# RWKV-7 recurrence with a four-expert mixture: the second inverse product moved into the first one's stretch, and three orders restated

## The chip, the cores and the metric

The kernel runs on one core of a Trainium2 chip. The metric is the device time of one execution in microseconds (us), as the median of several runs.

## What is computed

Inputs are r, k, v, w, a, b of shape (4, 8, 768, 40), and for the mixture domain_probs (3072, 4), w1 (4, 320, 1024) and w2 (4, 1024, 320), all in float32. Cut to what matters, the reference is:

```python
for t in range(S):                       # state: (B, H, D, D), starts at 0
    y[:, :, t] = einsum('bhd,bhde->bhe', rt, state)
    Sa = einsum('bhde,bhe->bhd', state, at)
    state = state * wt[:, :, None, :] - einsum('bhd,bhe->bhde', Sa, bt) \
            + einsum('bhd,bhe->bhde', vt, kt)
x = y.transpose(0, 2, 1, 3).reshape(B * S, H * D)
p = domain_probs / (domain_probs.sum(-1, keepdims=True) + 1e-09)
for e in range(4):
    out += p[:, e:e + 1] * (maximum(x @ w1[e], 0) @ w2[e])
```

## The kernel before

**Chunks and units.** The recurrence over time is done in chunks of 64 steps, so that most of it becomes matrix products. A unit is one chunk of two of the four batches (all 8 heads): 12 chunks times 2 pairs are 24 units, numbered u. Inside a chunk the steps depend on each other through a triangular system per head. Its inverse is put together from 32-wide blocks: the diagonal blocks are solved step by step on GpSimd, and two products join them.

**The parts of a unit** are Python generators, each yield being a place where another part can be put in between:

- `within` (L402) is what needs no state. y1: the decays are turned (`turn_raw`, tile rawW) and multiplied up by a scan (tile G, L439). y2: pg (TensorE transposes), then gp and its reciprocal on VectorE. y3: n_tok, k_tok, AT, VT, RT, on VectorE. y4: transposes pNT and pKT, copied by ScalarE. y5: the scores pc, masked into VC by VectorE (`causal`, L400). y6: the matrix F from pfe. y7: pe, masked into ET. y8: pev, copied into EV.
- `substitute` (L542) solves the diagonal blocks of F: copies into blocks (two on VectorE, two on ScalarE, L547), a transpose and two operations on M (VectorE), then 48 small operations on GpSimd (tile Z, L580 and L593).
- `merge` (L599) joins the blocks. y1: Qc and QTc (VectorE transposes of Z), and four copies into QT (GpSimd). y2: the first product pY with four ScalarE copies into Yq. y3: the second product pQ with four ScalarE copies into QT. Both products go through `two_heads` (L616).
- `step` (L636) brings in the state. y1: prn, then RH (VectorE sums, L654) and SN (ScalarE copies, L659). y2: psat with the copies SaT and SX. y3: pxr with the mask into SX and the copies RS. y4: pdy, the output Y and the new state. y5: Y goes to xT, for most chunks by 12 DMAs on SP (L744).

**The mixture** of a finished chunk (256 tokens) is a list `todo` of pieces, for each expert: ups(e, 0), down_1 of the expert before, ups(e, 1), and down_2 of the expert before with add_h of this one. An ups is `up_last` (64x64 tiles, 16 records) and `up_main` (128x128, 16 records), then a Relu on ScalarE into hs. `lead()` (L981) issues the up_last of the next piece ahead of the rest. down_1 and down_2 are products over hs and its sums (tiles p, 24 and 32 records), added with the gate into osb on VectorE (L789, L791). The piece list lags, so an up never reads an xT that was just made.

**Buffers.** PSUM has five banks for the recurrence (tag big) and three for the mixture (tag mm): an up takes two of the three, down_1 one, down_2 two.

**Order.** The loop over u (L1100) calls the generators of units u, u+1 and u+2 in turn, with `gap(n)` in between, which runs pieces of the mixture: two per gap from u = 5 on. From there on an iteration traces, on TensorE: pe(u+1), pxr(u), gap 0, pg(u+2), pev(u+1), pdy(u), gap 1, pNT, pKT and pc of u+2, prn(u+1), pY(u+1), gap 2, pQ(u+1), pf(u+2), lead, psat(u+1), gap 3. The planner of the language orders each engine's instructions by priority, which is the place in the code, and by readiness as it reckons it. An instruction given to `keep_in_program_order` is pinned behind everything that was traced on its engine before it. Matmuls go through `stated` (L70), which pins them where `in_order[0]` is true: in the preparation and for u up to 5 (L1101). `within` has a local `pin` that pins for the first units only. DMAs of weights are pinned on SP; `later` holds the 16 moves of rawV and rawR, given out in small portions after pieces of the mixture (`begin_later`, L965). TensorE's records stand under the helper's lines L76 (matmul) and L79 (transpose), so one goes by the tile names.

Of the kernel before, what the change touches and what calls it, by code (L numbers as in the profile page):

```python
# [1 line left out]

# [13 lines left out]
def kernel(  # L16
# [38 lines left out]
    nc = tc.nc  # L55

    B, H, S, D = r.shape
    E, DM, F = moe_w1.shape
    P = 128
    L = 64  # L60
    Q = 32
    NC = S // L
    NJ = H // 2
    NF = F // P
    NU = NC * B // 2
    DT = DM - 2 * P

    in_order = [False]
# [16 lines left out]
    def big(name):  # L85
# [6 lines left out]
        out=ident[:], in_=ident[:], pattern=[[1, P]], compare_op=ALU.is_equal, fill=0.0,  # L92
# [5 lines left out]
    for t, n, op in ((upf, L, ALU.is_gt), (diagf, Q, ALU.is_equal)):  # L98
        nc.vector.memset(t[:], 1.0)
        for q in range(P // n):  # L100
            o = slice(q * n, (q + 1) * n)
            nc.gpsimd.affine_select(
                out=t[o], in_=t[o], pattern=[[1, n]], compare_op=op, fill=0.0, base=0, channel_multiplier=-1,
# [75 lines left out]


    EARLY = 5

    class Unit:
        pass

    units = []

    def begin(u):
# [3 lines left out]
        q.start, q.end = q.c == 0, q.c == NC - 1  # L192
        q.apart = u >= EARLY + 2
        q.n = {}
# [44 lines left out]
    def turn_raw(out, t):  # L239

        return nc.vector.transpose(
            out=out.rearrange("p n (x two) -> p n two x", two=2),
            in_=t.rearrange("p n (two e) -> p n two e", two=2)[:, :, :, 0:Q],
        )
# [92 lines left out]
    def quarter(q):  # L337
        return slice(Q * q, Q * q + Q)

    def of_slot(x, s):  # L340

        return x.rearrange("p (j s) e -> p j s e", s=2)[:, :, s, :]
# [30 lines left out]
    def of_d_half(x, r):  # L373

        return x.rearrange("p (jj four) e -> p jj four e", four=4)[:, :, slice(1, 3) if r else slice(0, 4, 3), :]
# [7 lines left out]
    def quadrants(p, lo, order, out_cols, *terms):  # L383


        for j, s, i in order:
            for n, term in enumerate(terms):
                row, col, at, lhsT, rhs = term(j, s, i)
                matmul(
                    out=p[row][half(col), lo + at * out_cols:lo + (at + 1) * out_cols], lhsT=lhsT, rhs=rhs,  # L390
                    start=(n == 0), stop=(n == len(terms) - 1),
                )
        return [by(x[:, lo:lo + NJ * out_cols], out_cols) for x in p]

    def causal(to, data):
        mask = mask_up[:, None, :].to_broadcast([P, data.shape[1], L])
        if len(to.shape) == 4:
            mask = mask_up[:, None, None, :].to_broadcast([P, 2, 2, L])
            data = data.rearrange("p (jj two) t -> p jj two t", two=2)
        return nc.vector.copy_predicated(out=to, mask=mask, data=data)  # L400

    def within(q):  # L402

        n = q.n

        def pin(ins, also=False):
            if q.u <= PADDED or also:
                tc.keep_in_program_order(ins)
# [3 lines left out]
        q.G = Gv = G[:, 0:2 * NJ * L].rearrange("p (c t) -> p c t", t=L)  # L412
        ahead = G[:, 1:2 * NJ * L + 1].rearrange("p (j i t) -> p i j t", i=2, t=L)
        for i in range(2):
            pin(turn_raw(ahead[:, i], n["rawW"][:, NJ * i:NJ * i + NJ, :]))
        q.gl = sb.tile([P, 2 * NJ, 1], FP32, name="gl", tag="gl", bufs=4)
        pin(nc.vector.tensor_tensor(out=q.gl[:], in0=G[:, L::L][:, :, None], in1=first[:, :, 0:1], op=ALU.mult))
        pin(nc.vector.memset(Gv[:, :, 0:1], 0.0))
# [16 lines left out]
        if q.u == 1:  # L435
# [4 lines left out]
            out=G[:, 0:2 * NJ * L], data0=G[:, 0:2 * NJ * L],  # L440
# [22 lines left out]
        def causal_scores(VT):  # L463
            pc = quadrants(banks("pc"), 0, BY_TOKENS, L, lambda j, s, i: (
                d_half(j, s), i, j, of_slots(VT, d_half(j, s), j, i, D), of_slots(q.RT, d_half(j, s), j, i, D),
            ))
            for r in range(2):
                pin(causal(of_d_half(q.VC[:, :, D:D + L], r), pc[r]), q.start)

        q.K, q.N = k_tok(), n_tok()  # L470
        ins = nc.vector.scalar_tensor_tensor(
            out=q.N[:, :, 0:D], in0=n["B"][:], scalar=-1.0, in1=gp[:], op0=ALU.mult, op1=ALU.mult,
# [126 lines left out]
    def merge(q):  # L599


        Qc = sb.tile([P, H, Q], FP32, name="Qc", tag="q", bufs=2)
        QTc = sb.tile([P, H, Q], FP32, name="QTc", tag="q", bufs=2)
        tc.keep_in_program_order(nc.vector.transpose(out=dealt(Qc[:]), in_=q.Z))  # L604
        tc.keep_in_program_order(
            nc.vector.transpose(  # L606
                out=QTc[:].rearrange("p h r -> p (h r)"), in_=Qc[:].rearrange("p h c -> p (h c)"),
            )
        )
        q.QT = QTs()  # L610
        for i in range(P // Q):
            ins = nc.gpsimd.tensor_copy(out=q.QT[quarter(i), :, quarter(i % 2)], in_=QTc[quarter(i)])  # L612
            tc.keep_in_program_order(ins)
        yield

        def two_heads(name, lhsT, rhs, to):  # L616
            p = big(name)
            for n in range(NJ):
                for r in range(2):
                    matmul(  # L620
                        out=p[half(r), n * 2 * Q:(n + 1) * 2 * Q], lhsT=lhsT[half(r), 2 * n:2 * n + 2, :],
                        rhs=rhs[half(r), 2 * n:2 * n + 2, :], start=True, stop=True,
                    )
            for r in range(2):
                for y in range(2):
                    src = p[quarter(2 * r + y), 0:H * Q].rearrange("p (n two t) -> p n two t", two=2, t=Q)[:, :, y, :]
                    nc.scalar.copy(out=of_slot(to[quarter(2 * r)], y), in_=src)  # L627

        Y = Ys()
        two_heads("pY", q.below, QTc, Y)  # L630
        yield

        two_heads("pQ", Qc, Y, q.QT[:, :, quarter(1)])
        yield

# [327 lines left out]
    todo, last, later, stores = [], [], [], []  # L963

    def begin_later(n):  # L965
        for move in later[:n]:
            tc.keep_in_program_order(move(nc.sync))
        del later[:n]
# [12 lines left out]
    def lead():  # L981
        if todo and hasattr(todo[0], "lead"):
            todo[0].lead()

    def run(gen, n=99):
        if gen is None:
            return
        for _ in range(n):
            if next(gen, gen) is gen:
                break  # L990
# [19 lines left out]
    ws = [within(units[u]) for u in range(3)]  # L1010
# [24 lines left out]
    m, s = merge(units[0]), begin_step(0)  # L1035
# [38 lines left out]
    m, s = merge(units[1]), begin_step(1)  # L1074
# [23 lines left out]
    sums_at.update({4 * 4 + 3: 2, 4 * 5 + 0: 3, 4 * 5 + 1: 2, 4 * 5 + 2: 3})  # L1098
    sum_ops = (None for e in range(E) for _ in add_weights(e))
    for u in range(1, NU):  # L1100
        in_order[0] = u <= EARLY  # L1101
        q = units[u]
        m = s_next = w = w_next = iter(())
        if u + 1 < NU:
            m, s_next = merge(units[u + 1]), begin_step(u + 1)
            w_next = ws[u + 1]
        if u + 2 < NU:
            w = ws[u + 2]

        def gap(n, pieces=None):  # L1110
            at = 4 * u + n
            run(sum_ops, sums_at.get(at, 0))
            mix((1 if at in sparse else 2) if pieces is None else pieces)

        early = u < EARLY
        if early:
            begin_later(len(later))
        ahead = u + 3 < NU and u in range(EARLY, EARLY + 3)
        if ahead:
            go(load_raw(begin(u + 3), "W"))  # L1120
        if early:
            lead()
        run(w_next, 99 if early else 1)
        run(s, 1)
        gap(0)


        if early:
            run(s, 1)
        run(w, 1)  # L1130
        if not early:
            run(w_next)
            run(s)

        if early:
            run(w, 1)
            gap(1, 2 if u + 1 == EARLY else None)
            run(s)
        if u == 1:
            mixture_of_unit(q)  # L1140
        elif q.bp:
            mixture_of_chunk(units[u - 1:u + 1], chunks_x[q.c])
        if not early:
            begin_later(len(later))
            run(w, 1)
            run(m, 1)
            gap(1)

        if u + 3 < NU:
            go(load_raw(units[u + 3] if ahead else begin(u + 3), "A" if ahead else "WA"))  # L1150
            load(units[u + 3], "WBKV")
            later.extend(load_raw(units[u + 3], "VR"))
        run(w, 2)

        soon = u in (2, 3, 4)
        if soon:
            run(w, 1)
        if early:
            run(m, 1)
        else:  # L1160
            run(s_next, 1)
            run(m, 1)
        if soon:
            substitute(units[u + 2], nc.gpsimd)
        gap(2)

        if not early:
            run(m, 1)
        if not soon:
            run(w, 1)  # L1170
        if not early:
            lead()
            run(s_next, 1)
        if not soon and u + 2 < NU:
            substitute(units[u + 2], nc.gpsimd)
        if early:
            run(w, 1)
        if u + 3 < NU:
            ws.append(within(units[u + 3]))
            run(ws[u + 3], 1)  # L1180
        if early:
            run(m, 1)
            run(s_next, 1)
            run(m)
            gap(3, 1)
            run(s_next, 1)
        else:
            gap(3)
        s = s_next
    mix(len(todo))  # L1190
# [30 lines left out]
```

## Time and profile before

| | |
|---|---|
| median of 3 runs | 1102.67 us (1099.94 to 1104.25) |
| profiled execution | 1102.3 us |
| its span, first to last instruction | 1100.6 us |
| mean granted TensorE clock | 0.991 |
| busy PE, DVE, ACT, POOL | 1070.0, 756.6, 353.0, 502.9 us |
| chain that ended last, PE's share | 81% |
| DMA, mean over the span | 111 GB/s |

PE is TensorE's matmuls and PEld its weight loads, DVE is VectorE, ACT ScalarE, POOL GpSimd, SP the queue that issues DMAs. A line of a timeline gives the start and the duration in us, engine, source line, operation, output tile and input tiles, shapes and count, and in brackets the idle time just before it with what ended it. A line of waits gives engine and tile, what was waited for, the sum in us, the number of waits and the longest.

### The profile page before, as it was taken

What the parts mean: (1) busy time and instruction counts of PE and PEld (TensorE: products, weight loads), DVE (VectorE), ACT (ScalarE), POOL (GpSimd) and SP (SyncE); (2) the same over time, 40 slices, a digit from 0 to 9 for tenths busy, and PEclk for the clock granted to TensorE, in tenths of its full rate; (3) what the DMA queues carried; (4) which work ended last, traced back from release to release, by engine and by line L of the source; (5) the groups of instructions that cost most, each with busy time, mean ns of one, the idle gap of its engine ahead of it and who ended that gap; (6) DMA issues with size and microseconds to landing.
All of it is one profiled execution on the core that took longest, in us unless ns stands there. A gap on an engine that the chain in (4) does not pass through costs nothing.

```text
span 1100.6 us, 38528 instructions
## 1 busy us (share of the span) xinstructions
PE 1070.0 (97%) x16102; PEld 955.8 (87%) x16102; DVE 756.6 (69%) x1551; ACT 353.0 (32%) x956; POOL 502.9 (46%) x1274
## 2 busy tenths in 40 slices
PE   6799899999999999999999999999999999999998
PEld 6677788789998999898999989989998989988887
DVE  7766668887777776767767768767767677543343
ACT  2432444223233233243233242332332432321110
POOL 5106677753463653743734635636537437430000
PEclk9799999999999999999999999999999999999999
DMA  7776545425345363354353444443552532222320
GB/s 117 226 247 138 136 103 117 119 55 136 98 111 127 98 140 97 94 146 103 93 144 94 102 121 104 116 120 84 127 123 65 147 85 67 98 69 82 104 76 13
DMA packets 268868, 122.18 MB, mean 111 GB/s; under 512 B 213736, under 2 KB 242072, under 8 KB 268696
## 3 DMA queue, kind: packets, MB, share of 16 engines
q1 hardware_dynamic: 265416, 119.12, 43.0%
q8 instruction: 127, 2.08, 0.8%
q10 hardware_dynamic: 3280, 0.61, 0.3%
q14 instruction: 45, 0.37, 0.1%
HBM read 111.79 MB, written 3.93 MB: 105 GB/s over the span
## 4 chain that ended last, share of the span: by engine, by line
PE 81%; DVE 7%; POOL 5%; ACT 3%; issue 2%; DMA 1%; SPq 0%; ACTq 0%; DVEq 0%; POOLq 0%
PE ph L76 35%; PE p L76 28%; POOL Z L593 3%; PE pdy L76 3%; PE psat L76 2%; PE pxr L76 2%; POOL Z L580 2%; PE prn L76 1%; PE pfe L76 1%; PE pQ L76 1%; PE po L76 1%; PE pc L76 1%; DVE Z L590 1%; PE pY L76 1%; DVE M L553 1%
## 5 line engine op out<-in xcount | busy, mean ns | idle before, releaser
L76 PE MATMUL ph<-xT,w1p 128*128 128x256 f32 (+3 forms) x3040 | 446.3, 377 | 4.0 <-issue 3.9
L76 PEld LDWEIGHTS ph<-xT,w1p 64*64 64x64 f32 (+1 forms) x3040 | 338.5, 162 | 72.7 <-issue 29.0
L593 POOL TENSOR_TENSOR Z<-Z 128x31 f32<-128x31 f32 (+7 forms) x704 | 260.0, 369 | 55.2
L897 DVE TENSOR_TENSOR a<-hs 128x512 f32<-128x512 f32 x220 | 151.8, 707 | 104.7 <-ACT hs L778 104.7
L580 POOL TENSOR_TENSOR Z<-M,Z 128x62 f32<-128x62 f32 (+7 forms) x352 | 144.1, 409 | 132.3 <-DVE M L569 106.4
L778 ACT ACTIVATE hs<-ph 128x512 f32<-128x512 f32 (+1 forms) x208 | 115.3, 564 | 226.5 <-PE ph L76 225.4
L76 PE MATMUL p<-sums,a 128*128 128x160 f32 x1056 | 164.9, 299 | 0.0
L76 PEld LDWEIGHTS p<-sums,a 128*128 128x128 f32 x1056 | 152.8, 190 | 2.2
L791 DVE SCALAR_TENSOR_TENSOR osb<-p,gate,osb 128x320 f32<-128x320 f32 (+1 forms) x243 | 108.1, 481 | 57.8 <-PE p L76 53.6
L550 POOL COPY below<-F 32x256 f32<-32x256 f32 x48 | 22.8, 475 | 198.7 <-ACT F L506 197.0
L76 PE MATMUL p<-w,a 128*128 128x160 f32 x704 | 105.9, 301 | 0.2 <-ACT hs L778 0.2
L76 PE MATMUL p<-w,hs 128*128 128x160 f32 x704 | 102.9, 299 | 0.0
L76 PEld LDWEIGHTS p<-w,hs 128*128 128x128 f32 x704 | 100.2, 190 | 2.2
L76 PEld LDWEIGHTS p<-w,a 128*128 128x128 f32 x704 | 98.3, 190 | 3.0 <-ACT hs L778 3.0
L612 POOL COPY QT<-QTc 32x256 f32<-32x256 f32 x96 | 51.7, 539 | 76.9 <-DVE QTc L606 67.7
L553 DVE STREAM_TRANSPOSE M<-blocks 128x1024 f32<-128x1024 f32 x24 | 47.4, 1977 | 38.1 <-ACT blocks L547 37.9
L700 ACT COPY RS<-pxr 64x256 f32<-64x256 f32 x88 | 32.2, 366 | 105.2 <-DVE SX L400 43.1
L451 DVE RECIPROCAL gp<-gp 128x320 f32<-128x320 f32 x24 | 51.6, 2151 | 0.7
L535 ACT COPY EV<-pev 64x160 f32<-64x160 f32 x96 | 23.1, 286 | 89.7 <-PE pev L76 89.3
L604 DVE STREAM_TRANSPOSE Qc<-Z 128x256 f32<-128x256 f32 x24 | 15.0, 627 | 46.2 <-POOL Z L593 46.1
L627 ACT COPY QT<-pQ 32x128 f32<-32x128 f32 x96 | 24.6, 256 | 59.9 <-PE pQ L76 58.2
L659 ACT COPY SN<-prn 128x256 f32<-128x256 f32 x44 | 14.9, 372 | 78.6 <-DVE RH L654 78.6
(149 smaller groups left out, 1357.5 us busy)
## 6 DMA issues: line engine op xcount, KB each, us to landing
w1p<-in_moe_w_dram SPq DMA_DIRECT2D x95, 512.0 KB
w1p<-in_moe_w_dram SPq DMA_DIRECT2D x190, 64.0 KB
w<-in_moe_w_dram SPq DMA_DIRECT2D x4, 1280.0 KB
sums<-in_moe_w_dram SPq DMA_DIRECT2D x9, 512.0 KB
natW<-in_w_dram SPq DMA_DIRECT2D x48, 80.0 KB
natB<-in_b_dram SPq DMA_DIRECT2D x48, 80.0 KB
natK<-in_k_dram SPq DMA_DIRECT2D x48, 80.0 KB
out_dram<-osb SPq DMA_DIRECT2D x46, 80.0 KB
```

The source lines that it names most:

```text
L76: return stated(nc.tensor.matmul(**k))
L451: pin(nc.vector.reciprocal(out=gp[:], in_=gp[:]))
L535: nc.scalar.copy(out=of_slot(q.EV[half(p)], i ^ p)[:, :, 0:D], in_=pev[i][half(p)])
L553: ins = nc.vector.transpose(out=M[:], in_=cols)
L580: ins = eng.tensor_tensor(out=Z[:, 1:3, 0:n, j + 1:Q], in0=M[:, j:j + 2, None, j + 1:Q].to_broadcast([P, 2, n, m]), in1=Z[:, here, 0:n, j: ...
L593: eng.tensor_tensor(out=z[:, 0], in0=z[:, 0], in1=z[:, x], op=ALU.add)
L612: ins = nc.gpsimd.tensor_copy(out=q.QT[quarter(i), :, quarter(i % 2)], in_=QTc[quarter(i)])
L627: nc.scalar.copy(out=of_slot(to[quarter(2 * r)], y), in_=src)
L700: nc.scalar.copy(out=RS[half(s), x ^ s::2], in_=prs[x][half(s)].rearrange("p (j i) t -> p j i t", i=2),)
L778: nc.scalar.activation(out=h[:, i * HF // 2:(i + 1) * HF // 2, 0:n], in_=ph[i][:], func=ACTF.Relu,)
L791: nc.vector.scalar_tensor_tensor(out=to, in0=p, scalar=sc, in1=to, op0=ALU.mult, op1=ALU.add)
L897: nc.vector.tensor_tensor(out=t[:], in0=x, in1=y, op=op)
```

## The change

Five things are done, nearly all for u from 5 on.

1. **TensorE as stated**: `in_order[0]` is true for all u.
2. **Gap 1**: `lead()` is called, the next two pieces change places (down_1 comes before the rest of the up), and `merge` y1 (Qc, QTc, QT) is traced after the gap.
3. **The stretch before gap 2** is now pNT, pKT, pc, pY, prn, lead, pQ: `merge` y3 has come ahead of gap 2. Behind it `within(u+3)` y1 (the decay turn and scan) is traced, which stood before gap 3; its two turns are pinned from unit 8 on, so behind RH. For u = 1, prn and pY move ahead of pf and pe.
4. **Priority**: `sooner` lifts, by 200 places, the masking into VC (units from 7 on), the Yq copies, and the whole of `substitute`, which is called ahead of psat.
5. **Raw loads**: all moves left in `later` are issued before gap 3.

```diff
+    SOONER = 200
+    def sooner(wanted):
+        return tc.high_priority(offset=SOONER) if wanted else nullcontext()
...
-            pin(turn_raw(ahead[:, i], n["rawW"][:, NJ * i:NJ * i + NJ, :]))
+            pin(turn_raw(ahead[:, i], n["rawW"][:, NJ * i:NJ * i + NJ, :]), q.u > EARLY + 2)
...
-            for r in range(2):
-                pin(causal(of_d_half(q.VC[:, :, D:D + L], r), pc[r]), q.start)
+            with sooner(q.apart):
+                for r in range(2):
+                    pin(causal(of_d_half(q.VC[:, :, D:D + L], r), pc[r]), q.start)
...
-                    nc.scalar.copy(out=of_slot(to[quarter(2 * r)], y), in_=src)
+                    with sooner(name == "pY"):
+                        nc.scalar.copy(out=of_slot(to[quarter(2 * r)], y), in_=src)
...
-        in_order[0] = u <= EARLY
+        in_order[0] = True
...
         if not early:
             begin_later(len(later))
             run(w, 1)
+            lead()
+            todo[:2] = todo[1::-1]
+            gap(1)
             run(m, 1)
-            gap(1)
...
         if early:
             run(m, 1)
         else:
+            run(m, 1)
             run(s_next, 1)
+            lead()
             run(m, 1)
+            if u + 3 < NU:
+                ws.append(within(units[u + 3]))
+                run(ws[u + 3], 1)
         if soon:
             substitute(units[u + 2], nc.gpsimd)
         gap(2)
 
-        if not early:
+        if u == 1:
+            run(s_next, 1)
             run(m, 1)
         if not soon:
             run(w, 1)
+        if not soon and u + 2 < NU:
+            with sooner(not early):
+                substitute(units[u + 2], nc.gpsimd)
         if not early:
             lead()
             run(s_next, 1)
-        if not soon and u + 2 < NU:
-            substitute(units[u + 2], nc.gpsimd)
         if early:
             run(w, 1)
-        if u + 3 < NU:
+        if early:
             ws.append(within(units[u + 3]))
             run(ws[u + 3], 1)
-        if early:
-            run(m, 1)
-            run(s_next, 1)
+            if u > 1:
+                run(m, 1)
+                run(s_next, 1)
             run(m)
             gap(3, 1)
             run(s_next, 1)
         else:
+            begin_later(len(later))
             gap(3)
```

More of the change, by code (lines that the diff above doesn't have):

```diff
@@ L1 @@
-from contextlib import ExitStack
+from contextlib import ExitStack, nullcontext
 import concourse.bass as bass
```

## The prediction

> **What bounds the kernel now.** I read the page first, then TensorE's own waits, then the timelines of iteration u = 13 (from pe at 567.8 us to the next pe at 610.7 us).
>
> ```profile
> PE 1070.0 (97%) x16102; PEld 955.8 (87%) x16102; DVE 756.6 (69%) x1551; ACT 353.0 (32%) x956; POOL 502.9 (46%) x1274
> PE   6799899999999999999999999999999999999998
> PEclk9799999999999999999999999999999999999999
> ```
> TensorE is busy in every slice from about 250 us to the end, at full granted clock. By windows, PE is busy 675.28 of the 676.00 us from 267 to 943. So most of the time is work that the change keeps. What can go are waits that hide inside busy PE, and a few open ones before 267 us. TensorE's waits from 267 to 943:
>
> ```profile
> PEld p L76 <- ACT hs L778: 3.0, 13, 0.4
> PEld ph L76 <- PE pfe L76: 1.1, 2, 0.9
> PE ph L76 <- issue: 0.5, 1, 0.5
> ```
> The first is the one that repeats: 13 of 17 iterations, 0.23 us each. Its cause is on ACT and DVE:
>
> ```profile
> 590.86 1.32 DVE L439 TENSOR_TENSOR_SCAN G<-G,first 128x512 f32<-128x512 f32 x1
> 592.32 1.58 DVE L791 SCALAR_TENSOR_TENSOR osb<-p,gate,osb 128x320 f32<-128x320 f32 x4
> 593.82 0.76 DVE L400 COPY_PREDICATED VC<-mask_up,pc 128x256 f32<-128x256 int32 x2
> 595.82 0.55 DVE L654 TENSOR_TENSOR RH<-prn,EV 128x160 f32<-128x160 f32 x2
> ```
> ```profile
> 596.17 0.65 ACT L659 COPY SN<-prn 128x256 f32<-128x256 f32 x2 [4.20 <-DVE RH L654]
> 596.83 0.79 ACT L627 COPY Yq<-pY 32x128 f32<-32x128 f32 x3
> 597.65 1.09 ACT L778 ACTIVATE hs<-ph 128x512 f32<-128x512 f32 x2
> 605.59 0.81 ACT L547 COPY blocks<-F 32x256 f32<-32x256 f32 x2
> ```
> RH (the sum on prn) stands behind the next unit's decay scan and down_1's adds; ACT stands 4.20 us in front of SN; the three late Yq copies and then the Relu of the gap's hidden layer queue behind; the second accumulator of down_2 waits for a PSUM buffer that this Relu frees:
>
> ```profile
> 597.12 2.53 PE L76 MATMUL p<-w,a 128*128 128x160 f32 x16
> 600.67 0.62 PE L76 MATMUL pQ<-Yq,Qc 64*64 64x64 f32 x13
> ```
> The same 16 records take 2.34 us elsewhere, so about 0.2 us is stall. The last line above it (605.59) shows blocks after SaT and SX copies: the solve on POOL starts late and ends just in time, since DVE's Qc waits for it (next line) and pY follows 2.1 us after Qc starts.
>
> ```profile
> 588.92 0.63 DVE L604 STREAM_TRANSPOSE Qc<-Z 128x256 f32<-128x256 f32 x1 [2.38 <-POOL Z L593]
> ```
>
> [...]PEld is at 87%, PE at 97%, and the 3.0 us above stands under PEld while PE shows no idle.[...]
>
> **The change, part by part**, in us from pNT's start (588.63) unless said otherwise.
>
> *Order of TensorE.* In the trace the late PE order is already that of the code (pe pxr, gap 0, pg pev pdy, gap 1, pNT pKT pc prn pY, gap 2, pQ pf lead psat, gap 3), so pinning it costs nothing by itself. Its price is that no other piece fills in when an operand is late. The number of 128-to-64 switches stays four per iteration: 0.
>
> *Swap in gap 1.* After pdy come lead (0.95), down_1 (3.26), then the main part of up (3.65). down_1 needs a PSUM buffer beside lead's two: the last add of gap 0 ends at -8.85 (gp starts right after it), the buffer is needed about -7.0: 1.9 us to spare. a1 has been ready since gap 0. Its four adds on DVE (1.6 us) run 3.65 us earlier, out of RH's way. up's weights load goes 3.26 us later on SP; behind it are natB, natK and raw loads that now start at +6 or later anyway: 0.
>
> *pQ into the stretch.* Qc and QTc are pinned behind down_1's adds. Unit data of DVE (k_tok) end at -2.06 or -2.82, by turns; adds 1.6, Qc and QTc 1.05: QTc at +0.6 or -0.2. pY wants it at 0.44 + 0.53 + 0.51 = 1.48: 0.9 to spare. Z must then be done by about -0.5 (next part). Yq: pY ends 1.84, first copy about 2.05, four of 0.26 to 3.1. pQ comes after prn (0.93) and lead (0.87), at 3.64: 0.5 to spare; so ACT's work is hidden by these two, and without them it would cost 1.3 us as in iteration 1. One new wait: five PSUM buffers serve pNT, pKT, two pc, pY; prn's second bank must take pKT's, which ACT frees at 0.74 + 0.48 + 0.59 = 1.81, where prn wants it at 1.84. Bounds 0 and 0.1 us each; I take 0.06, 17 times: +1.0. pQ itself needs pc's buffer, and the copies into VC (0.76) now have priority: done by 2.4.
>
> *Scan behind RH.* Two turns of 0.41, gl 0.19, memset 0.07, scan 1.32, gl 0.18: 2.6 us of DVE leave RH's front; they issue no DMA, and rawW landed long before. RH follows prn at 2.9, SN at 3.6, the Relus come when gap 2's matmuls end. pg of that unit is 30 us later. The 0.23 us stalls go: **-3.0**. With QT copied by 5.3, psat (13.4) no longer comes 0.1 us behind it; psat to ph varies from 1.08 to 1.43, over its low end summed 1.4: **-1.4**. pf likewise, 0.53 to 0.62, summed: **-0.6**. Lead behind pf, the second line of waits: **-1.0** (its larger case, 0.9, in iteration 7).
>
> *Blocks with priority.* ACT's two copies (0.81) go ahead of SaT and SX, right after F: F ends about 13.9 (pQ's 0.4 is gone before it), M starts about 14.9 instead of 17.8. POOL's chain ends near -2.6 instead of +0.3. SaT and SX come 0.8 us later, hidden by gap 3 (6.9 us) before pxr.
>
> *Raw loads (SP).* The ten moves left are flushed before gap 3, 10 x 0.44 = 4.4 us of SP, ahead of its w1p load, which waits for gap 3's up anyway. DVE's waits for rawV (2 us) shrink; off the path: 0.
>
> *Iteration 1.* prn and pY go ahead of pf and pe, which then cover Yq: pQ's open wait of 1.33 goes but for some 0.4 (Yq's four copies against 1.0 us of pf, pe): **-0.9**. The wait for RT of unit 7 (0.94 at 246) stays.
>
> Sum: -3.0 - 1.4 - 0.6 - 1.0 - 0.9 + 1.0 = -5.9 us. Against the profiled execution (1102.3 us, span 1100.6) that is 1096.4; its median of runs is 1102.67, so 1096.8 there.
>
> **Rivals.**
> *A, the gain is eaten (1101).* For: pKT's buffer has no slack at all, and pQ's margin is 0.5 us, in an order that can no longer bend. If ACT holds NT back by 0.25 us more behind up's last Relu, prn waits 0.3 per iteration: -5.9 + 17 x 0.25 = -1.7. Against: ACT is busy 32%.
> *B, slower (1115).* QTc comes late. It decides from 1.4 us after pNT: pinned behind the adds, it also waits for whatever the planner puts before them on DVE. The AT turn and product (1.38 us, today behind VC) would bring QTc to 1.2 and 2.0; with 0.7 us of a DMA wait (today DVE waits 1.4 to 2.4 us for rawV) to 1.9 and 2.7, so pY stalls 0.5 and 1.3, on average 0.9, and the shortened slack on DVE adds pev's and psat's operands for perhaps 0.2 more: 17 x 1.1 = 18.7 on 1096.8. Against: DVE stood idle 1.4 to 2.4 us before Qc, and all of it must be used up first.
> *C, nothing moves (1102).* Steady PE order is the code's already; if the 0.23 us only moves to another buffer, the time stays with iteration 1's 0.9.
>
> **How the numbers follow.** A measurement of this kernel tells about 0.5% (5.5 us) from no change. Forecast case (1094 to 1099): 0.62, of which about 0.42 lies under 1097.2. A and C: 0.20. B: 0.18. So faster 0.42, same 0.40, slower 0.18. Low end: all waits gone, no new one, 1095.8, less the 2 us by which runs differ, 1093.5. High end: A with twice its stall, 1106; that leaves out B and the tail.
>
> **What would show it.** PEld's wait p <- hs falls from 3.0 us to near 0; the iteration falls from 42.84 to about 42.5 us; SN no longer waits 4 us for RH; blocks on ACT before SaT; Qc waits for the adds and not for POOL; prn waits 0.1 us or less. Wrong if pY waits for QTc, prn for KT, or pQ for Yq by more than 0.3 us in most iterations.

## The result, and the profile after

| | before | after |
|---|---|---|
| median | 1102.79 us (1099.94 to 1104.69, 7 runs) | 1096.73 us (1096.05 to 1099.56, 7 runs) |
| ratio to before | | 0.9949, 95% interval 0.9933 to 0.9965 |
| profiled execution, its span | 1102.3, 1100.6 us | 1096.91, 1095.2 us |
| mean granted TensorE clock | 0.991 | 0.988 |

Put in again later beside other kernels (as e10), the changed kernel took 1097.37 us, ratio 0.9933 (0.9914 to 0.9951). The forecast was 1096.8 us.

The page of after, busy times and slices, then the line of the chain that ended last:

```profile
PE 1068.1 (98%) x16102; PEld 959.0 (88%) x16102; DVE 759.0 (69%) x1551; ACT 353.4 (32%) x956; POOL 490.3 (45%) x1274
...
PE   7798999999999999999999999999999999999998
...
PEclk8799999999999999999999999999999999999999
...
PE 92%; DVE 4%; ACT 1%; DMA 1%; issue 1%; SPq 0%; DVEq 0%; ACTq 0%
```

Busy PE fell by 1.9 us only, and the time by 5.4: most of the work is the same. POOL was 5% of the chain before and is no longer in it, so the chain no longer runs through the solve.

TensorE's waits in after, among all from 267 to 943 us (engine and tile, what was waited for, sum, times, longest): the one of its matmuls, two of its weight loads, and the two that the prediction named on ACT and DVE.

```profile
PEld ph L76 <- issue: 6.5, 15, 1.1
...
PEld p L76 <- issue: 6.2, 16, 0.4
...
ACT SN L665 <- DVE RH L660: 5.7, 16, 0.4
...
PE ph L76 <- issue: 0.7, 1, 0.7
...
DVE Qc L609 <- POOL Z L598: 0.2, 1, 0.2
```

The same two of ACT and DVE in before:

```profile
ACT SN L659 <- DVE RH L654: 65.0, 16, 4.5
...
DVE Qc L604 <- POOL Z L593: 35.7, 16, 2.5
```

The line p <- hs (3.0 us, 13 times) is gone. A line p <- issue of 6.2 us stands there now and costs nothing: down_2 takes 4.44 us in all 16 iterations, where it took 4.64 to 4.86 in 13 of them. These weight loads wait while matmuls still run, and nothing is lost; what tells the two cases apart is the length of the group.

DVE and ACT in iteration 13 of after; its pNT starts at 586.34 us:

```profile
582.73 0.56 DVE L481 TENSOR_TENSOR k_tok<-natK,gp 128x320 f32<-128x320 f32 x1
583.22 1.58 DVE L797 SCALAR_TENSOR_TENSOR osb<-p,gate,osb 128x320 f32<-128x320 f32 x4
584.72 0.62 DVE L609 STREAM_TRANSPOSE Qc<-Z 128x256 f32<-128x256 f32 x1
585.37 0.45 DVE L611 STREAM_TRANSPOSE QTc<-Qc 128x256 f32<-128x256 f32 x1
588.08 0.78 DVE L404 COPY_PREDICATED VC<-mask_up,pc 128x256 f32<-128x256 int32 x2 [2.26 <-PE pc L76]
...
589.62 0.52 DVE L660 TENSOR_TENSOR RH<-prn,EV 128x160 f32<-128x160 f32 x2
...
591.35 1.23 DVE L443 TENSOR_TENSOR_SCAN G<-G,first 128x512 f32<-128x512 f32 x1
```
```profile
588.50 1.07 ACT L633 COPY Yq<-pY 32x128 f32<-32x128 f32 x4 [0.40 <-PE pY L76]
589.94 0.65 ACT L665 COPY SN<-prn 128x256 f32<-128x256 f32 x2 [0.36 <-DVE RH L660]
...
600.13 0.81 ACT L552 COPY blocks<-F 32x256 f32<-32x256 f32 x2
601.31 0.65 ACT L681 COPY SaT<-psat 128x256 f32<-128x256 f32 x2 [0.37 <-PE psat L76]
```

The adds come straight behind k_tok, QTc ends 0.53 us before pNT starts, the scan stands behind RH, SN waits 0.36 us where it waited 4.20, and blocks go ahead of SaT. TensorE in the same iteration:

```profile
587.82 0.57 PE L76 MATMUL pY<-QTc,below 64*64 64x64 f32 x13
...
590.09 0.63 PE L76 MATMUL pQ<-Yq,Qc 64*64 64x64 f32 x16
...
595.29 2.34 PE L76 MATMUL p<-w,a 128*128 128x160 f32 x16
```

pY starts 1.48 us after pNT, as soon as its turn comes, and the 16 records that took 2.53 us take 2.34.

### The profile page after: what moved, and what is told of

It reads as the page before. It is cut to its first block, busy times and chain, and to the rows that moved or that the text cites. A ratio compares the mean times of both kernels' runs of the same rounds, so it can differ in the third digit from the quotient of the medians.

```text
span 1095.2 us, 38536 instructions
## 1 busy us (share of the span) xinstructions
PE 1068.1 (98%) x16102; PEld 959.0 (88%) x16102; DVE 759.0 (69%) x1551; ACT 353.4 (32%) x956; POOL 490.3 (45%) x1274
## 4 chain that ended last, share of the span: by engine, by line
PE 92%; DVE 4%; ACT 1%; DMA 1%; issue 1%; SPq 0%; DVEq 0%; ACTq 0%
PE ph L76 39%; PE p L76 31%; PE pdy L76 3%; PE psat L76 2%; PE pxr L76 2%; PE po L76 2%; PE prn L76 2%; PE pfe L76 1%; PE pc L76 1%; PE pQ L76 1%; PE pev L76 1%; PE pg L79 1%; PE pY L76 1%; DVE Z L595 1%; PE pe L76 1%
## 5 line engine op out<-in xcount | busy, mean ns | idle before, releaser
L598 POOL TENSOR_TENSOR Z<-Z 128x31 f32<-128x31 f32 (+7 forms) x704 | 254.8, 362 | 55.2
L585 POOL TENSOR_TENSOR Z<-M,Z 128x62 f32<-128x62 f32 (+7 forms) x352 | 148.6, 422 | 99.0 <-DVE M L574 73.1
L76 PE MATMUL p<-w,a 128*128 128x160 f32 x704 | 102.8, 299 | 0.0
L617 POOL COPY QT<-QTc 32x256 f32<-32x256 f32 x96 | 40.4, 421 | 81.9 <-DVE QTc L611 68.7
L404 DVE COPY_PREDICATED VC<-mask_up,pc 128x256 f32<-128x256 int32 x48 | 18.7, 442 | 45.4 <-PE pc L76 45.3
L511 ACT COPY F<-pfe 128x256 f32<-128x256 f32 x48 | 15.5, 376 | 80.9 <-PE pfe L76 79.3
L76 PE MATMUL pdy<-VC,k_tok 64*64 64x104 f32 (+1 forms) x768 | 38.2, 259 | 0.0
```

The lines of the kernel that those rows point to most:

```text
L76: return stated(nc.tensor.matmul(**k))
L585: ins = eng.tensor_tensor(out=Z[:, 1:3, 0:n, j + 1:Q], in0=M[:, j:j + 2, None, j + 1:Q].to_broadcast([P, 2, n, m]), in1=Z[:, here, 0:n, j: ...
L598: eng.tensor_tensor(out=z[:, 0], in0=z[:, 0], in1=z[:, x], op=ALU.add)
```

## The experiments

Times of each kernel against the kernel before on the same chip (1104.55, 1103.23, 1104.23 and 1103.10 us in its four turns):

| | median, us | ratio, 95% interval |
|---|---|---|
| e1 scan alone, on before | 1099.6 | 0.9957 (0.9942 to 0.9972) |
| e2 without the scan's pin | 1115.37 | 1.0097 (1.0076 to 1.0118) |
| e3 without the swap | 1139.93 | 1.0326 (1.0304 to 1.0347) |
| e4 pQ into the stretch alone, on before | 1129.1 | 1.0224 (1.0206 to 1.0242) |
| e5 solve behind psat | 1138.91 | 1.0329 (1.0306 to 1.0352) |
| e6 iteration 1 in its old order | 1098.01 | 0.9953 (0.9937 to 0.9969) |
| e7 raw loads not flushed | 1101.72 | 0.9987 (0.9977 to 0.9998) |
| e8 weights among the xT transfers | 1097.99 | 0.9940 (0.9926 to 0.9955) |
| e9 as e8, iteration 1 old | 1096.47 | 0.9928 (0.9912 to 0.9944) |
| e10 the change again | 1097.37 | 0.9933 (0.9914 to 0.9951) |
| e11 rawA early | 1099.15 | 0.9951 (0.9931 to 0.9970) |
| e12 as e11, iteration 1 old | 1097.15 | 0.9939 (0.9922 to 0.9956) |

Iterations are counted from pe(u+1) to the next pe from u = 6 on, and from one pg to the next for u up to 5. From u = 8 on the changed kernel takes 42.41 and 42.57 us by turns, the kernel before 42.84 on average.

My theory of the gain: RH stood behind the scan on DVE, and everything else in the change is there to make room or costs nothing. Rivals: the second product's place is what pays; and rivals A and B of the prediction.

### e1: the scan's move alone

```diff
-            pin(turn_raw(ahead[:, i], n["rawW"][:, NJ * i:NJ * i + NJ, :]))
+            pin(turn_raw(ahead[:, i], n["rawW"][:, NJ * i:NJ * i + NJ, :]), q.u > EARLY + 2)
...
             run(s_next, 1)
+            if u + 3 < NU:
+                ws.append(within(units[u + 3]))
+                run(ws[u + 3], 1)
...
-        if u + 3 < NU:
+        if early:
```

> The kernel before with one part of the change alone: within y1 (decay turn and scan) of unit u+3 is traced behind prn's sums instead of ahead of gap 3, and its two turns are pinned there from unit 8 on. Theory (the stall in gap 2 comes from RH standing behind the scan, so that SN, Yq and the Relu are late): RH leaves 2.6 us earlier, at about 5 us after pNT, the Relu of gap 2 starts near 6.5, down_2's second accumulator finds its buffer free; the 0.26 us per iteration over 16 iterations goes: about 1098.5 us, down_2 4.44 us instead of 4.70. Rival (the gain comes from the solve on GpSimd that starts earlier, which this kernel leaves as it was): no change, 1102.8 us.

1099.6 us, 4.95 less than the kernel before in the same turn; the whole change took off 6.06 us, and 6.86 as e10. As expected, down_2 is 4.44 us in every iteration, and of the repeated wait two cases are left from 267 us on (267 to 940):

```profile
PEld p L76 <- ACT hs L778: 1.3, 2, 1.0
...
PE ph L76 <- issue: 1.1, 1, 1.1
```

So a piece of one of the five parts, laid on the kernel before, brings most of the gain; its interval overlaps that of the whole change. From pNT to psat the 16 iterations from 267 us get 2.7 us shorter together, against 3.2 in the whole change, and the steady iterations take 42.47 and 42.61 us by turns. In this one profile two other waits hide a part of it: iteration 7 takes 44.14 us (43.52 in before; see e8), and iteration 18 takes 43.66, with a wait of 0.79 us for hs in gap 0. So the 16 iterations are 1.6 us shorter than in before, where those of after are 4.4 shorter.

### e2: the change without the pin of the scan's turns

```diff
-            pin(turn_raw(ahead[:, i], n["rawW"][:, NJ * i:NJ * i + NJ, :]), q.u > EARLY + 2)
+            pin(turn_raw(ahead[:, i], n["rawW"][:, NJ * i:NJ * i + NJ, :]))
```

> The changed kernel without the pin on the two decay turns (units from 8 on). The order on VectorE then has turns and scan ahead of down_1's adds, and Qc, pinned behind the adds, 2.6 us later; all other orders are those of the changed kernel. Theory (rival B of the prediction is real and it is this pin that keeps it away): scan from -3 to -0.4 us after pNT, adds to 1.2, QTc at 2.3 instead of -0.5; pY, wanted at 1.48, stalls about 0.9 us in each of some 14 iterations: about 1109 us. Rival (QTc has room enough, the pin does nothing): 1096.7 us.

1115.37 us, above the estimate, in the direction expected. The scan's turns go ahead of Qc on DVE. From unit 11 on QTc ends 2.14 to 2.18 us after pNT, where pY wants it at 1.48. Waits from 267 to 940:

```profile
PE pY L76 <- DVE QTc L611: 10.5, 15, 1.3
```

This is rival B's mechanism with another instruction in front of QTc than the one named, and it comes out at B's 1115 us. The 15 waits are 10.5 us, and the 16 iterations from 267 us are 13.1 us longer than in after. The profile as a whole is 18.6 us longer: 4.6 of that lie in iteration 5, where pc also waits 2.96 us for RT. That the total meets B's figure is therefore in part chance.

### e3: the change without the swap in gap 1

```diff
-            todo[:2] = todo[1::-1]
```

> The changed kernel with gap 1 in its old order (up before down_1; lead still ahead). Theory (the swap is what lets Qc stand behind the adds): p431 ends at pNT's start, its adds take VectorE to 1.8 us, Qc, the masks into VC and QTc follow to 3.6; pY stalls 2.1 us and pQ with it, in 17 iterations: about 1133 us. Rival (the swap is only a change of places, since TensorE does the same work): 1097 us.

1139.93 us. In iteration 13 down_1's adds start 0.21 us after pNT instead of 3.12 ahead of it, Qc and QTc stand behind them, and QTc ends 3.25 us after pNT (267 to 943):

```profile
PE pY L76 <- DVE QTc L611: 26.0, 15, 1.7
```

The steady iteration is 44.37 and 44.52 us by turns. So the swap costs nothing, as the prediction had it, and it is needed: without it the adds stand in QTc's way, and the kernel is 3.3% slower than the kernel before.

### e4: only pY, prn, lead and pQ ahead of gap 2, on the kernel before

```diff
+            run(m, 1)
             run(s_next, 1)
+            lead()
+            run(m, 1)
...
-        if not early:
-            run(m, 1)
```

> The kernel before with one part alone: pY, prn, lead and pQ ahead of gap 2, nothing else. Theory (pQ must wait for pc's PSUM buffers, and the masks that free them stand behind the scan and the adds on VectorE): masks end near 6.1 us after pNT, pQ wanted at 3.6 stalls 2.5 us, in 17 iterations, less the 4 us of the stall in gap 2: about 1140 us. Rival (the move of pQ is itself the gain): 1097 us.

1129.1 us; the direction was right, the size too large. It is VC's masks that are late, not QTc: they end 6.05 us after pNT, and pQ, which takes the PSUM buffer of pc, starts at 5.86 instead of 3.75 (267 to 940):

```profile
PE pQ L76 <- DVE VC L400: 23.0, 14, 1.7
```

So the second product's place is not what pays: alone it loses 24.6 us. In the change the masks end 2.52 us after pNT, with the scan and the adds out of their way. What this move adds inside the whole change was not tested apart and stays open; the scan's move brings most of the gain without it.

### e5: the solve behind psat, without priority

```diff
-        if not soon and u + 2 < NU:
-            with sooner(not early):
-                substitute(units[u + 2], nc.gpsimd)
         if not early:
             lead()
             run(s_next, 1)
+        if not soon and u + 2 < NU:
+            with sooner(False):
+                substitute(units[u + 2], nc.gpsimd)
```

> The changed kernel with the solve's call back behind psat and without its priority. ScalarE's order is then SaT, SX, blocks, and VectorE's has VT, which waits for the raw loads, ahead of M. Theory (starting the solve early is needed, as Qc is wanted at 1.4 us after pNT): M waits for rawV and rawR, starts near -21 instead of -28 us, GpSimd's chain of 25 us ends near +4, pY stalls some 4 us, in 17 iterations: about 1160 us; if VT's load lands in time, GpSimd ends at +0.3 as before and it is 1099 us. Rival (the solve has slack in any place): 1096.7 us.

1138.91 us, between the two outcomes that were given. Iterations of about 49 and of 42.58 us alternate. In the long ones M starts 21 us before pNT, Z ends 4.45 us after it and QTc 5.57; in the short ones M starts at -25.0 and QTc ends at 1.46. Waits of the span from 267 to 943:

```profile
PE pY L76 <- DVE QTc L611: 22.8, 7, 4.1
```

By these numbers M must start some 25 us ahead of pNT, an estimate; the change starts it at -27.8. In the compiled programs the order is the same on every engine with and without the priority on the solve: it is the place of the call, ahead of psat, that does it. The same holds for the priority of VC's masks; of the three only that of the Yq copies alters the compiled program.

### e6: the change with iteration 1 in its old order

```diff
-        if u == 1:
-            run(s_next, 1)
-            run(m, 1)
...
-            if u > 1:
-                run(m, 1)
-                run(s_next, 1)
+            run(m, 1)
+            run(s_next, 1)
```

> The changed kernel with iteration 1 in its old order (pf, pe, pY, prn, pQ). Theory (from the profiles so far: iterations 1 to 3 took 97.6 to 98.0 us in three kernels with the new order, 95.3 to 96.7 in three with the old, so what pQ no longer waits is lost again behind it): 1.8 us shorter than the changed kernel, about 1095 us. Rival (the prediction's term of -0.9 is right): 0.9 us longer, 1097.6 us.

1098.01 us, not to be told from the change, so the expected 1.8 us did not come. In the profile iterations 1 to 3 took 94.9 us, 2.7 less than in after, but iterations 6 and 7 took 43.89 and 47.34 us instead of 42.68 and 43.75: what was gained early was gone at the lead of gap 3.

### e7: the change without the flush of raw loads ahead of gap 3

```diff
         else:
-            begin_later(len(later))
             gap(3)
```

> The changed kernel without the flush of the raw loads ahead of gap 3. Theory (it is off the path; RT then comes as the last of y3, 0.7 us before down_1's adds, within QTc's slack of 1.9 us): no change within 0.5 us, about 1096.7. Rival (late raw loads reach pc through RT, as in iteration 5): 1 us or more longer.

1101.72 us, over 22 runs: 4 to 6 us of the gain are gone, and the interval doesn't meet that of the change. The profile does not show where. It is 1.5 us longer than after's up to 267 us, but iteration 4 alone is 1.95 longer, at a clock of 0.81 in the stretch from 207 to 216 us (last section), which other kernels have too. Of the 1.9 us behind 267, 0.8 lie in iterations 6 and 7, which differ as much between two profiles of the changed kernel itself (86.43 us in after, 87.33 in e10). The rest are three iterations with 0.3 to 0.5 us more around the lead and up of gap 3. The rival's size came, but not its way: pc has no wait for RT from 267 to 943 us. e1 has no flush either and is at 0.9957, below this kernel's interval; so it is together with the other parts that the flush is needed.

### e8 and e9: is it the weights?

First theory of iteration 7's wait: the lead waits for w1p, which SP issues behind twelve xT transfers. The edit puts gap 1's load between them:

```diff
+            if h == 5 and q.u >= EARLY:
+                yield
             lo = h * D
...
-            run(s)
+            run(s, 2)
...
             gap(1)
+            run(s)
             run(m, 1)
```

> The changed kernel with one more edit: from unit 5 on, of the twelve transfers of Y into xT the first six are issued before gap 1 and the other six behind it, so that gap 1's load of up weights (w1p) stands between them on SP, not behind all twelve. Nothing else is changed. Theory: the lead of gap 3 waits in iteration 7 (0.7 us at 344) because these weights are issued by SP only at 26.5 to 28.2 us after pe. Then the load is issued from about 21 us on, the wait in iteration 7 goes, iteration 7 falls from 43.75 to about 42.6 us, and the time falls by about 1 us, to 1095.5. The small alternation at gap 3 (4.58 and 4.74 us) may go too: at most another 1.3 us. Rival: in that iteration the lead reads the xT that has just been made, and it is xT that is late. Then the last xT transfers are issued about 1.7 us later (at 27.5), the wait grows to about 2 us, and other odd iterations wait too: about 1100.

> The same edit on the kernel in which iteration 1 has its old order. That kernel reached unit 6 some 2 us earlier than the changed one and lost it at gap 3 of iterations 6 and 7 (43.89 and 47.34 us instead of 42.6). Theory of the late weights: both waits go, the 2 us are kept, and the time is about 1094 us, the best of all. Rival (xT itself is late, or something else in gap 3 is bound to a fixed time): iterations 6 and 7 stay at or above 43.9 and 47 us, and the time stays at 1098 or more.

> The changed kernel as it is, on the same chip as the two kernels beside it, to set their few microseconds against. Expected 1096.7 us, 0.9949 of the kernel before; in its profile, iterations 1 to 3 at 97 to 98 us, iteration 7 at 43.75 us, the later ones at 42.41 and 42.57 us by turns.

1097.99, 1096.47 and 1097.37 us; in e10 iterations 1 to 3 took 97.6 us and iteration 7 43.89, close to what was expected. On SP the load moved ahead of the last transfers in iteration 6 only; it seems that a pin ties an instruction to the one traced just before it on its engine, which is narrower than "everything before it" above. In iteration 6 the load's issue began 25.0 us after pe in e8 and 24.5 in e9, instead of 25.6 in after; yet the lead, which does not wait there in after, now waited 0.83 us in e8 and 0.09 in e9. Iteration 7, where the order on SP is the old one, took 44.99 us in e8 (43.75 in after) and 43.80 in e9 (47.34 in e6): one longer, one shorter. So the theory of the weights falls, and so does the forecast of 1094 us for e9.

What holds the lead is read on DVE. In after, iteration 7, DVE, then TensorE:

```profile
340.16 0.71 DVE L245 STREAM_TRANSPOSE AT<-rawA 128x512 f32<-128x512 f32 x1 [3.85 <-DMA rawA<-in_a_dram]
...
342.72 0.54 DVE L797 SCALAR_TENSOR_TENSOR osb<-p,gate,osb 128x320 f32<-128x320 f32 x1
...
343.78 0.37 DVE L797 SCALAR_TENSOR_TENSOR osb<-p,minus_gate,osb 128x160 f32<-128x160 f32 x1
```
```profile
344.26 0.87 PE L76 MATMUL ph<-xT,w1p 64*64 64x256 f32 x11 [0.71 <-issue]
```

The AT turn of unit u+3 stands on DVE and waits 3.85 us for its raw data; behind it is an add of down_2 (the line at 343.78), which by the times below frees the lead's second PSUM buffer. Nothing else runs on DVE in these 3.85 us, and where the turn no longer waits (e11, below) the add ends at 32.47 us after pe instead of 34.80. The profile gives the wait as "issue", so it can be seen only from the times: the add ends at 34.80 us after pe and the lead goes on at 34.91; in e6 36.84 and 36.94, in e8 36.06 and 36.16, in e1 35.20 and 35.30. From iteration 8 on the turn starts at 23.43, the add ends at 32.47, and the lead goes on when its turn comes, at 33.61. The turn waits 5.68 us in e6, 5.08 in e8 and 3.89 in e9: how late rawA lands sets how long iteration 7 is.

### e11 and e12: rawA ahead of the xT transfers

```diff
         if ahead:
-            go(load_raw(begin(u + 3), "W"))
+            go(load_raw(begin(u + 3), "WA"))
...
-            go(load_raw(units[u + 3] if ahead else begin(u + 3), "A" if ahead else "WA"))
+            go(load_raw(units[u + 3] if ahead else begin(u + 3), "" if ahead else "WA"))
```

> The changed kernel with one edit: in iterations 5, 6 and 7 the raw moves of a (rawA) for unit u+3 are traced with those of w at the start of the iteration, not behind gap 1. On SP they then stand ahead of the twelve transfers of Y into xT. The order of TensorE, ScalarE and GpSimd is the same. Theory: what held the lead of gap 3 back in iteration 7 was neither w1p nor xT. It was DVE, where the AT turn of unit u+3 stands waiting 3.8 us for rawA (it starts at 30.8 us after pe, later ones at 23.4), and behind it stands down_2's last add on p75, which frees the lead's second PSUM buffer: the add ends at 34.80, the lead goes on at 34.91 (e6: 36.84 and 36.94, e8: 36.06 and 36.16). Then the turn starts near 23.4 in iterations 6 and 7, the add ends near 32.5, the lead does not wait, iteration 7 falls from 43.75 to about 42.6 us, and the time by 1 to 1.5 us, to about 1095.5. Rival (weights or xT late): the lead still goes on at 34.5 or later in iteration 7, and it stays at 43.7 us.

> The same edit on the kernel in which iteration 1 has its old order, whose iterations 6 and 7 took 43.89 and 47.34 us. Theory of the late rawA: both fall to about 42.5, and the 2 us gained in iterations 1 to 3 are kept: about 1093 us, 0.991 of the kernel before, and below the change as it is. Rival: the two iterations stay long (43.9 and 47), and the time stays at 1097 or more.

1099.15 and 1097.15 us. The mechanism is as stated: in both kernels iterations 6 and 7 are 42.41 and 42.57 us, the turn no longer waits, the add ends at 32.47. The gain in time did not come. One cause can be read: in iteration 5 the early AT turn and its product now stand ahead of RT on DVE (e11):

```profile
246.86 0.67 DVE L245 STREAM_TRANSPOSE AT<-rawA 128x512 f32<-128x512 f32 x1
247.56 0.89 DVE L485 TENSOR_TENSOR AT<-AT,G 128x512 f32<-128x512 f32 x1
248.37 0.70 DVE L245 STREAM_TRANSPOSE RT<-rawR 128x512 f32<-128x512 f32 x1
```

pc waits 1.35 us for RT there (1.36 in e12), the iteration from 236.9 to 280.4 us takes 43.5 where after takes 42.2, and the one before it has a lower clock as well, in both (last section). No version is shown to beat the change: the intervals of e6, e9 and e12 overlap with its own.

## Why the prediction was right, and where not

The prediction's terms against the two profiles, each summed over the 16 iterations from 267 us, in us:

| term | predicted | measured |
|---|---|---|
| gap 2's stall (down_2, 74.39 to 71.06) | -3.0 | -3.3 |
| psat behind QT (psat to up, 18.80 to 17.83) | -1.4 | -1.0 |
| pf (8.96 to 8.24) | -0.6 | -0.7 |
| lead behind pf (14.71 to 14.78) | -1.0 | +0.1 |
| prn for pKT's buffer | +1.0 | +0.8 |
| other pieces of these iterations | 0 | -0.3 |
| before 267 us (iteration 1, RT) | -0.9 | -0.6 |
| after the last of them | 0 | -0.4 |
| sum | -5.9 | -5.4 |

**Right, mechanism and size.** The scan behind RH. 13 stalls of 0.23 us were read where PE shows none, from a group that took 2.53 instead of 2.34 us; e1 shows that this one move ends them and brings most of the gain. prn's new wait, bounded between 0 and 0.1 us and taken at 0.06, is 0.05 (0.93 to 0.98). The cover that the swap gives to QTc (e3), the margin of QTc (e2) and the solve's start (M 14.9 us after pNT expected, 14.6 measured) are as worked out. Rival A did not come: pQ starts 3.75 us after pNT in all 16 iterations, 3.64 expected. Rival B exists: it is one pin away (e2). Rival C's "Steady PE order is the code's already" holds too: in the compiled programs TensorE's order in the kernel before is the same with `in_order` true throughout, and in the changed one without it, so the first of the five parts does nothing. Two small slips don't bear on this: the window from 267 to 943 us holds 16 iterations, not 17, and by the terms given the range would be 1093.8 to 1105.3.

**Failed: "Lead behind pf, the second line of waits: -1.0 (its larger case, 0.9, in iteration 7)".** The step put the wait down to pf, since the profile named it, and took it to go with psat's waits. Iteration 7 took 43.52 us before and 43.75 after. Its cause is the AT turn's wait for rawA on DVE (e11: gone with rawA early), which the change doesn't touch.

**Failed: "The wait for RT of unit 7 (0.94 at 246) stays".** It went, and iteration 5 fell from 43.3 to 42.2 us. DVE before, then after; the osb lines are down_1's adds:

```profile
243.20 1.23 DVE L439 TENSOR_TENSOR_SCAN G<-G,first 128x512 f32<-128x512 f32 x1
...
244.56 1.01 DVE L791 SCALAR_TENSOR_TENSOR osb<-p,gate,osb 128x320 f32<-128x320 f32 x2
245.48 0.70 DVE L241 STREAM_TRANSPOSE RT<-rawR 128x512 f32<-128x512 f32 x1
```
```profile
242.28 1.58 DVE L797 SCALAR_TENSOR_TENSOR osb<-p,gate,osb 128x320 f32<-128x320 f32 x4
...
244.43 0.45 DVE L611 STREAM_TRANSPOSE QTc<-Qc 128x256 f32<-128x256 f32 x1
244.79 0.67 DVE L245 STREAM_TRANSPOSE RT<-rawR 128x512 f32<-128x512 f32 x1
...
249.63 1.23 DVE L443 TENSOR_TENSOR_SCAN G<-G,first 128x512 f32<-128x512 f32 x1
```

The scan and the adds both stood ahead of RT, and both have moved. In e1 only the scan has moved, and the wait is as long as before; DVE, then TensorE:

```profile
243.91 1.01 DVE L791 SCALAR_TENSOR_TENSOR osb<-p,gate,osb 128x320 f32<-128x320 f32 x2 [2.55 <-PE p L76]
244.83 0.70 DVE L241 STREAM_TRANSPOSE RT<-rawR 128x512 f32<-128x512 f32 x1
```
```profile
245.68 0.69 PE L76 MATMUL pc<-RT,VT 40*64 40x64 f32 x32 [0.94 <-DVE RT L241]
```

The adds wait for down_1, and RT stands behind them. In e3, which has everything but the swap, pc waits 0.94 us again. So the swap removed this wait: it brings down_1 and its adds forward. The prediction priced the swap for RH and QTc only, at 0; RT stands behind the same adds and gains 1.0 us.

That the sum came so near is in part luck. The errors of the lead (+1.1) and of RT (-1.0) have nothing to do with each other and nearly cancel. The two profiles also had their lower clock in different places: before's in iteration 4, after's in iterations 1 to 3 (next paragraph).

**Failed: iteration 1, "-0.9".** pQ's wait of 1.33 us fell to 0.22, but iterations 1 to 3 took 97.6 us (95.3 before); the next wait, of up's main part at about 126 us, is 1.58 us now (1.32). The clock (below) is mixed in, so profiles of like clock have to be set side by side. With 1.00 in the stretch from 96 to 110 us iterations 1 to 3 took 94.8 to 95.8 us in the old order (four profiles) and 95.9 and 96.5 in the new one; with 0.88 to 0.91 they took 96.5 and 96.7 in the old and 97.2 to 98.0 in the new one (six). So the new order is about 1 us longer there, not 0.9 shorter. Iteration 4 fell from 43.1 to 40.7 us, but it takes 40.6 to 41.2 in the old order too where the clock is full (e1, e4, e6, e9): before's profile was slow there. To the whole time the order makes no difference that e6 could show.

**Failed: raw loads, "off the path: 0".** Without the flush the changed kernel is 4 to 6 us slower (e7). The prediction looked at DVE's waits for rawV only and found them covered; at which transfer the cost arises stays open.

## What to carry to other kernels

Here a stall of 0.23 us in each of 13 iterations showed as a longer group (2.53 us instead of 2.34) and a weight-load wait, not as idle time of the bound engine; follow such a stall back through the order of each engine, and one moved instruction may be most of the gain (4.95 of 6.06 us in e1). Price a moved instruction for everything that stands behind it on its engine, in every iteration, not only for the consumer that it was moved for: here RT gained 1.0 us that way. Where two instructions that were moved stood ahead of a third, a run with one of them moved alone tells which of them held it. The wait of 0.71 us in iteration 7 that the profile calls "issue" was by its times one for a PSUM buffer, freed by an add that stood on DVE behind a turn waiting 3.85 us for a transfer: where such a wait has no cause in the profile, look on the other engines for an instruction that waits for a transfer and isn't needed yet.

## What the runs showed of the hardware

Behind a short wait of TensorE the granted clock was lower in some of these runs, and the records there took longer. Iteration 4 before and after, the same 30 records, then the window behind the wait in before and, behind a wait of 2.74 us, in e6 (columns: stretch, length, busy PE, PEld, DVE, ACT, POOL with counts, granted clock, DMA share, GB/s):

```profile
209.56 6.38 PE L76 MATMUL ph<-xT,w1p 64*64 64x256 f32 x30 [2.09 <-issue]
```
```profile
211.56 4.74 PE L76 MATMUL ph<-xT,w1p 64*64 64x256 f32 x30 [1.30 <-issue]
```
```profile
209.50:216.00 6.50, 6.44 (x34) 4.64 (x36) 6.29 (x13) 0.62 (x2) 5.17 (x9) 0.74 0.65 111
```
```profile
344.60:348.00 3.40, 3.32 (x76) 2.73 (x78) 3.28 (x7) 0.00 (x0) 0.00 (x0) 0.50 0.73 216
```

In before the clock is 1.00 from 200 to 209 us and 0.74 from 209.5 to 216; in after it is 1.00 from 200 to 216. So of iteration 4's 2.4 us, 0.8 are wait (2.09 against 1.30) and 1.6 are the longer time of the same 30 records (6.38 against 4.74) at the lower clock. Not every such wait was followed by a lower clock, and some shorter ones were. The same wait of iteration 4 is 1.49 to 1.52 us long in nine profiles; the clock in the stretch from 207 to 216 us is 0.81 to 0.85 in three of them (e7, e11, e12) and 1.00 in the other six. The wait for RT near 105 us, 1.6 to 1.9 us long in all 14 profiles, goes with a clock of 0.88 to 0.91 in the stretch from 96 to 110 us in eight of them and with 1.00 in six; in after, one of the eight, it is 1.00 from 96 to 103.5 us and 0.67 from 105.4 to 110, behind the wait. Of the eight two have the old order of iteration 1, of the six four; these are too few to say whether the order matters.

Why the clock fell behind some of these waits and not behind others is not shown.
